# One fused attention and mixture-of-experts kernel: transposing transfers moved behind the maxima's, stacking and splitting of maxima moved forward, gates copied six steps behind a fetch

## The chip, the cores and the metric

The kernel runs on one NeuronCore of a Trainium2 chip, as one launch. The metric is the device time of that launch in microseconds, lower is better. Three runs of the kernel before took 1018.86, 1014.24 and 1013.54 us; their median, 1014.24 us, is the time before. One more execution was taken by the hardware profiler and took 1015.18 us. All profile lines below are from that one.

A core has five engines with an instruction queue each, worked off in order: PE (TensorE, matmuls; its weight loads are shown as PEld), DVE (VectorE), ACT (ScalarE), POOL (GpSimd) and SP (SyncE, which here only issues transfers). ACT and POOL issue transfers too. All transfers share 16 DMA engines.

## The reference

The inputs are `q`, `k` and `v` of 8 batches, 8 heads, 576 tokens and 64 features, a scalar `tau` = 0.02, and the gate and expert weights.

```python
scores = scale * np.matmul(q, k.transpose(0, 1, 3, 2))
thresh = np.max(scores, axis=-1, keepdims=True) - tau
scores = np.where(scores >= thresh, scores, -1000000000.0)
attn   = softmax(scores);  out = np.matmul(attn, v)
x      = out.transpose(0, 2, 1, 3).reshape(4608, 512)
expert_idx = np.argmax(x @ w_gate, axis=1)        # one of 8 experts
y[t] = gate_w[t] * relu(x[t] @ w1[expert]) @ w2[expert]
```

So each row of scores keeps only the entries within `tau` of its maximum, and each of the 4608 tokens goes to one of 8 experts, whose hidden layer is 1024 wide. The row maximum must be exact enough that the comparison keeps the same entries, and the choice of the expert must not flip. Therefore the operands are split into pairs of half-precision numbers (a high part and a rest) that are multiplied together.

## The kernel before

**Attention.** The work is cut into 32 pairs of heads, four pairs to a batch, and each pair into 10 steps. One step of the program issues, for a pair `n`, a unit of transposed scores (`st`, lines 335 and 336) with exponential (ACT) and mask (DVE), for an earlier pair a piece of attention times values (`av`, lines 408 to 419), and for a later pair a unit of plain scores (`s`, lines 286 and 288), of which DVE takes the negated row maxima (`nm`, lines 293 and 298). The plain scores run 20 steps ahead of the transposed ones.

**Maxima.** When a pair's plain scores are done, `parts` reduces the maxima to `r` (line 305); three steps later PE transposes them (`pst`, line 309), and ACT and DVE in turn split them into three half-precision parts `ptT` (lines 314 to 317), one operation a step. Three small transfers on SP (line 323) put these parts as three more rows into `CQ`, one of the operands of line 336. So the first `st` unit of a pair can't start before they have landed. The tiles of `pst`, of the logits (`lg`), of the ranks (`rk`) and of the expert counts (`pc`) share one PSUM buffer.

**Stacking.** `split` makes high and low parts of a pair's q and k (ACT, then POOL for `lo`, line 223), and `stack` writes them with 13 transfers on SP (lines 237 to 252) into `QK`, `ck` and `CQ`, four buffers each. `SL` (8) sets how many steps ahead of the plain scores that happens; loading and splitting hang on the same number.

**Batch end and routing.** After a batch's fourth pair, `finish` sets up: transposing transfers of the batch's rows `R` on SP (line 499, `xTg`; four of them, and a fifth for the half block `Rh` of an odd batch), the logits (line 519) on PE, `route` (DVE, lines 526 to 554), `ranks` (lines 575 to 592), and then the sending of each block of rows to its place in DRAM by indirect transfers on POOL (line 596, `xs`). `R` has two buffers, so batch b+2 writes (ACT line 470, POOL line 467) into what batch b sends from.

**Experts.** `level` makes tables of rows on DVE after batches 5, 6 and 7. `fetch` (line 799) gathers a group's 128 rows from `xs` by an indirect transfer on POOL, transposes them by a transfer on SP (line 805, `xTm`), and copies the gate (DVE, line 808, `gt`) and the target row (POOL, line 813). Groups 0, 1 and 2 can be fetched after batch 5 and groups 3 and 4 after batch 6; from group 5 on, the sends of batch 7 must have been made. `gemm1` (line 850) and `gemm2` (line 877) do the expert's two layers, fed by weights that SP loads (line 752, `wf`) and ACT and DVE split (lines 765 and 766, `wb`).

**What sets the order.** `after(k, f, where)` puts an action k steps on, at one of three places (FRONT, MID, END) of the step; each engine gets its instructions in the order in which the steps emit them. That holds up to 16 steps before the end of the attention. What is emitted later is ordered by a scheduler's own estimate of time, and may be put among the last written-out steps.

Of the kernel before, what the change touches and what calls it, by code (L numbers as in the profile page):

```python
# [11 lines left out]
F32 = mybir.dt.float32  # L12
# [3 lines left out]
ALU = mybir.AluOpType  # L16
# [3 lines left out]
B, H, S, D = 8, 8, 576, 64  # L20
DM, E, F = 512, 8, 1024
# [22 lines left out]
CAP = NTOK  # L44

TUNE = dict(
    lead=10, cast=1, sl=8, ll=15, sp0=6, sps=0, lv=-9, sv=-2, av=2, tr=4, d=2, lg=5, d5=2, d6=2, d7=1, lg7=9, km=16, rate=15, dh=1, do=3, ws0=6, wsd=3, w1d=5, plv=1, xv=3, so=0, sto=0, ord=0, sc=5, fa=3, fd=4, wa1=-70, wa2=-86, wl1=-28, wl2=-6, avb=2, route=1, ranks=7, pp=8, ew=4, maskat=0, w1a=-40, w1b=3,
)


# [1 line left out]
def kernel(  # L52
# [9 lines left out]
    nc = tc.nc  # L62
# [9 lines left out]
    ew = ctx.enter_context(tc.tile_pool(name="ew", bufs=4))  # L72
# [8 lines left out]
    pp = apool.enter_context(tc.tile_pool(name="pp", bufs=5))  # L81
# [93 lines left out]
    FRONT, MID, END = range(3)  # L175

    def plan(k, f, where=END):
        assert (k, where) >= (now[0], slot[0])
        acts.setdefault(k, ([], [], []))[where].append(f)

    def after(k, f, where=END):
        plan(now[0] + k, f, where)

    def phase(p, least):

        return least + (p - now[0] - least) % NSTEP if now[0] + least < KM else least
# [113 lines left out]
    def parts(n):  # L300


        nm = st[n]["nm"]
        r = small.tile([P, 9], F32, tag="r", name=f"r_{n}")
        nc.vector.tensor_reduce(r, nm.rearrange("p a t -> p t a"), axis=AX.X, op=ALU.min)

        def turn():
            ps = ps_m.tile([P, 512], F32, tag="m", name=f"pst_{n}")
            nc.tensor.transpose(ps[0:9, 0:P], r, ident)
            x, y = ps[0:9, 0:P], ps[0:9, P:2 * P]  # L310
            t = small.tile([9, 3, P], F16, tag="ptT", name=f"ptT_{n}", bufs=1)
            v, a = nc.vector, nc.scalar
            for i, f in enumerate((
                lambda: a.activation(t[:, 0], x, AF.Identity, bias=thr[0:9]),
                lambda: v.scalar_tensor_tensor(y, x, thr[0:9], t[:, 0], ALU.add, ALU.subtract),
                lambda: a.copy(t[:, 1], y),
                lambda: (v.tensor_tensor(t[:, 2], y, t[:, 1], ALU.subtract), rows(t)),
            )):
                after(1 + i, f, MID)

        def rows(t):
            for p in range(3):
                nc.sync.dma_start(
                    st[n]["CQ"][64 + p:65 + p].rearrange("p (t c) -> p t c", t=9), t[:, p]
                )

        after(3, turn, FRONT)
# [57 lines left out]
    def row(b, j):  # L385
        return Rs[b % 2][:, j] if j < NT else Rh[b // 2 % 2]

    def halves(x):
        return x.bitcast(F16).rearrange("p (c h d) -> p c h d", c=4, h=2)
# [35 lines left out]
    def divide(x, y, rs, eng):  # L425
        wait = int(eng is nc.gpsimd)
        nc.scalar.activation(rs, y[..., D:W].squeeze(y.ndim - 1), AF.Copy, bias=EPS)
        after(wait, lambda: nc.vector.reciprocal(rs, rs))
        after(2 * wait, lambda: eng.tensor_tensor(
            x, y[..., 0:D], rs.unsqueeze(rs.ndim).to_broadcast(list(x.shape)), ALU.mult  # L430
        ))
# [43 lines left out]
    def finish(b):  # L475
        last = b == B - 1
        n = NT + b % 2
        xTs = {}

        def lone():  # L480
            o = halves(Rh[b // 2 % 2][:, 0:DM])
            y = xhs[b // 2 % 2]
            rs = small.tile([P, H], F32, tag="rsh", name=f"rsh_{b}", bufs=1)
            xn = xp.tile([P, H, D], F32, tag="xn", name=f"xnh_{b}", bufs=2)
            x = xn.rearrange("p (c u) d -> p c (u d)", c=4)
            eng = nc.vector if last else nc.gpsimd
            divide(xn, y, rs, eng)

            def high():
                nc.scalar.copy(o[:, :, 0], x)  # L490
                after(1, lambda: eng.tensor_tensor(o[:, :, 1], x, o[:, :, 0], ALU.subtract))

            after(1 if last else 4, high)

        def turn(j):
            if j % 2 == 0:
                xTs["t"] = rpool.tile([P, 2, 8, P], F16, tag="xT", name=f"xTg_{b}_{j}", bufs=3)
            xTs[j] = xT = xTs["t"][:, j % 2]
            nc.sync.dma_start_transpose(xT, row(b, j)[:, 0:DM].bitcast(F16))

        if n > NT:
            after(1 if last else 2, lone)
        t0 = 2 if last else TUNE["tr"] + 3
        for j in range(n):
            after(t0 + j, lambda j=j: turn(j))
        d = t0 + n - 1
        dist = TUNE[f"d{b}"] if b >= B - 3 else TUNE["d"]
        after(
            d + TUNE["lg7"] if last else phase(7, d + TUNE["lg"]), lambda: logits(b, n, xTs, dist),
            END if last else FRONT,  # L510
        )
# [256 lines left out]
    def late(m):  # L768
        return m == "x" or m >= NEARLY

    def fetch(m):

        idx, bad, par = slots[m]
        g, i = group_of[m] if m != "x" else ((m,), 0)
        if m in range(NF, NF + 2):

            Rm = row(B - 2, m - NF)
            at = 4 * ROW - (2 - (m - NF)) * DM
            xT = Rs[B % 2].rearrange("p j c -> p (j c)")[:, at:at + DM].bitcast(F16)
            xT = xT.rearrange("p (i c t) -> p i c t", i=1, c=8)  # L780
        elif m in range(NF):
            Rm = pools[0].tile([P, ROW], I32, tag="Rm", name=f"Rm_{m}", bufs=2)
            xT = pools[0].tile([P, 1, 8, P], F16, tag="xTm", name=f"xTm_{m}", bufs=NF)
        else:
            Rm = row(B - 1, 0 if m == "x" else m % 5)
            if i == 0:
                xT = rpool.tile([P, 2, 8, P], F16, tag="xT", name=f"xTm_{m}", bufs=3)
            else:
                xT = ms[g]["xT"]
        if i == 0:  # L790
            ms[g] = dict(xT=xT, par=par, gw=[], ti=[])
        d = ms[g]
        for z in range(1 + late(m)):
            dst = xT[:, i]
            if late(m):
                Rm = row(B - 1, z if m == "x" else (2 * m + z) % 5)
                dst = xT.rearrange("p i c t -> p (i c t)")[:, 0:8 * PL].rearrange("p (c t) -> p c t", c=8)
                d["xT"], dst = dst, dst[:, :, P * z:P + P2 * z]
            dma = nc.gpsimd.indirect_dma_start(
                Rm, None, xs[:, :], bass.IndirectOffsetOnAxis(ap=idx[:, z:z + 1].bitcast(U32), axis=0)  # L800
            )
            for x in sends:
                tc.add_manual_dep(dma.ins, x.name, SYNC)
            tc.add_to_no_dep_group("xs", dma.ins)
            nc.sync.dma_start_transpose(dst, Rm[0:P2 if z else P, 0:DM].bitcast(F16))
            gt = small.tile([P, 2], I32, tag="gt", name=f"gt_{m}_{z}", bufs=6)
            gw, ti = gt.bitcast(F32)[:, 0:1], gt[:, 1:2]
            nc.vector.tensor_copy(gw, Rm.bitcast(F32)[:, DM:DM + 1])
            to = Rm[:, DM + 1:DM + 2]
            if z:  # L810
                nc.gpsimd.tensor_tensor(ti, to, to, ALU.add)
                to = ti
            nc.gpsimd.tensor_tensor(ti, to, bad[:, z:z + 1], ALU.add)
            d["gw"].append(gw)
            d["ti"].append(ti)

# [162 lines left out]
    def tables0():  # L979
        T[0], _ = level(0, ((), EARLY[0]), None)  # L980
        for m in range(NF):
            after(1 + m, lambda m=m: fetch(m))

    def tables1():
        T[1], _ = level(1, EARLY, T[0])
        for m in range(2):
            after(1 + m, lambda m=m: fetch(NF + m))
# [43 lines left out]
    for i in range(8):  # L1031
        plan(k + WS0 + WSD * i, lambda i=i: split_w(*wseq[i]))
        if i + 2 < 8:
            plan(k + WS0 + WSD * i, lambda i=i: load_w(*wseq[i + 2]))
    TABLES = {B - 3: tables0, B - 2: tables1, B - 1: tables2}
    plan(KEND + 12, close)

# [26 lines left out]
    for e in range(1, E + NL):  # L1064
        for w in range(2):
            for c in range(4):
                i = 4 * w + c
# [11 lines left out]
    turn = [8]  # L1079
# [88 lines left out]
    with tc.For_i(NL, total) as m:  # L1168
        idx = small.tile([P, 2], I32, tag="idx", name="idx_x", bufs=1)
        nc.vector.tensor_copy(idx.unsqueeze(1), T["row"][:, ds(m, 1)])  # L1170
        bad = small.tile([P, 2], I32, tag="badx", name="bad_x", bufs=1)
# [66 lines left out]
```

## Time and profile before

| What | Value |
|---|---|
| Median of three runs | 1014.24 us |
| Profiled execution, whole time | 1015.18 us |
| Its span, first to last instruction | 1013.0 us |
| Mean TensorE clock that was granted | 0.977 of full |
| PE busy with matmuls | 927.9 us |
| DVE, ACT, POOL busy | 652.6, 611.4, 556.5 us |
| HBM traffic over the span | 108 GB/s |

A timeline row gives the start, the duration, the engine, the line, the operation with output and inputs, and in brackets how long the engine stood idle before and what released it. "SPq" and "ACTq" are transfers being issued by the queue of SP or ACT; their duration is the time of issue, not of the transfer. A row of the waits reads: engine and line, what it waited for, the total in us, how often, and the longest. A row of the windows gives, for a stretch of time, the busy us and the number of instructions of each engine, the granted clock of PE (1.00 is full speed), the busy share of the DMA engines and GB/s.

### The profile page before, as it was taken

What the parts mean: (1) busy time and instruction counts of PE and PEld (TensorE: products, weight loads), DVE (VectorE), ACT (ScalarE), POOL (GpSimd) and SP (SyncE); (2) the same over time, 40 slices, a digit from 0 to 9 for tenths busy, and PEclk for the clock granted to TensorE, in tenths of its full rate; (3) what the DMA queues carried; (4) which work ended last, traced back from release to release, by engine and by line L of the source; (5) the groups of instructions that cost most, each with busy time, mean ns of one, the idle gap of its engine ahead of it and who ended that gap; (6) DMA issues with size and microseconds to landing.
All of it is one profiled execution on the core that took longest, in us unless ns stands there. A gap on an engine that the chain in (4) does not pass through costs nothing. (4 is left out here: it accounts for less than half of the span.)

```text
span 1013.0 us, 25162 instructions
## 1 busy us (share of the span) xinstructions
PE 927.9 (92%) x10027; PEld 657.6 (65%) x10027; DVE 652.6 (64%) x1309; ACT 611.4 (60%) x1036; POOL 556.5 (55%) x477
## 2 busy tenths in 40 slices
PE   2799999989999799899798699699999999999997
PEld 1266767657767567676576587387766676667684
DVE  6798888868888688888687675725341433423550
ACT  2588888858888678788587564324342433423641
POOL 5378788958979779789585671441212122122121
PEclk9899999989999899999899899899999999999999
DMA  6554474754746646647446749988564755557720
GB/s 174 134 122 108 110 166 118 164 122 130 171 112 161 130 115 174 147 127 163 113 127 154 123 167 286 313 176 225 173 175 153 228 154 172 156 158 219 226 104 26
DMA packets 181715, 158.96 MB, mean 157 GB/s; under 512 B 137561, under 2 KB 153947, under 8 KB 181596
## 3 DMA queue, kind: packets, MB, share of 16 engines
q1 hardware_dynamic: 129244, 100.35, 40.0%
q10 hardware_dynamic: 43200, 27.53, 10.6%
q0 software_dynamic: 9152, 29.45, 8.8%
q8 instruction: 80, 1.31, 0.6%
q14 instruction: 39, 0.32, 0.1%
HBM read 90.24 MB, written 19.44 MB: 108 GB/s over the span
## 5 line engine op out<-in xcount | busy, mean ns | idle before, releaser
L372 POOL TENSOR_TENSOR pl<-e,ph 128x1024 f16<-128x1024 f32 x95 | 204.8, 2157 | 63.4 <-ACT ph L371 61.9
L298 DVE TENSOR_REDUCE nm<-s 128x1 f32<-128x512 f32 (+1 forms) x320 | 200.1, 636 | 61.0 <-PE s L288 59.1
L850 PEld LDWEIGHTS <-wb 128*128 128x128 f16 x2304 | 190.2, 99 | 29.3 <-issue 11.4
L850 PE MATMUL h<-xTm,wb 128*128 128x256 f16 (+2 forms) x2112 | 196.7, 255 | 10.1 <-DMA xTm<-R 10.1
L877 PE MATMUL y<-wb,hl 128*128 128x512 f16 (+1 forms) x1056 | 201.5, 360 | 0.0
L363 ACT ACTIVATE e<-st,ntau 128x512 f32<-128x512 f32 x192 | 130.8, 683 | 55.3 <-PE st L336 53.4
L877 PEld LDWEIGHTS <-hl 128*128 128x128 f16 (+1 forms) x1056 | 94.1, 100 | 98.1 <-issue 1.9
L286 PE MATMUL s<-QK 128*128 128x512 f16 (+3 forms) x640 | 138.2, 293 | 14.2 <-DMA QK<-lo 13.5
L766 DVE SCALAR_TENSOR_TENSOR wb<-wf,wb 128x1024 f16<-128x1024 f32 x96 | 116.7, 1252 | 52.0 <-ACT wb L765 49.6
L336 PE MATMUL st<-CQ,ck 128*128 128x512 f16 (+3 forms) x640 | 133.7, 290 | 16.3 <-DMA CQ<-ptT 16.3
L288 PE MATMUL s<-ck,CQ 128*128 128x512 f16 (+3 forms) x640 | 142.6, 291 | 4.8 <-DMA ck<-lo 4.4
L335 PE MATMUL st<-QK 128*128 128x512 f16 (+3 forms) x640 | 138.4, 293 | 8.6 <-DVE e L348 6.4
L366 DVE SCALAR_TENSOR_TENSOR e<-st,e 128x512 f32<-128x512 f32 x192 | 129.7, 676 | 8.6 <-ACT e L363 5.8
L891 POOL DMA_INDIRECT out_dram<-o,gt x40 | 43.6, 1089 | 150.1 <-ACT o L888 139.4
L347 ACT ACTIVATE e<-st,ntau_f 128x512 f32<-128x512 f32 (+1 forms) x160 | 93.5, 602 | 53.6 <-PE st L336 53.4
L838 ACT ACTIVATE hl<-h 128x512 f16<-128x512 f32 (+1 forms) x80 | 45.8, 573 | 125.3 <-PE h L850 125.3
L414 PE MATMUL av<-vf,e 128*128 128x65 f32 (+1 forms) x1024 | 118.7, 254 | 0.0
L765 ACT ACTIVATE wb<-wf 128x1024 f16<-128x1024 f32 x96 | 97.4, 1049 | 19.8 <-PE h L850 8.8
L348 DVE SCALAR_TENSOR_TENSOR e<-st,e 128x512 f32<-128x512 f32 (+1 forms) x160 | 91.6, 589 | 20.2 <-ACT e L347 20.1
L414 PEld LDWEIGHTS av<-vf,e 128*128 128x128 f32 (+1 forms) x1024 | 104.0, 167 | 0.4
L371 ACT CAST ph<-e 128x1024 f16<-128x1024 f32 x96 | 99.3, 1034 | 1.7 <-DVE e L366 1.7
L417 PE MATMUL av<-vop,ph 128*128 128x64 f16 x768 | 97.4, 194 | 0.0
(193 smaller groups left out, 1493.3 us busy)
## 6 DMA issues: line engine op xcount, KB each, us to landing
wf<-in_w_dram SPq DMA_DIRECT2D x96, 512.0 KB
qkf<-in_qk_dram ACTq DMA_DIRECT2D x30, 576.0 KB
vf<-in_v_dram ACTq DMA_DIRECT2D x30, 320.0 KB
QK<-hi SPq DMA_DIRECT2D x64, 144.0 KB
QK<-hi SPq DMA_DIRECT2D x64, 72.0 KB
QK<-lo SPq DMA_DIRECT2D x64, 72.0 KB
ck<-lo SPq DMA_DIRECT2D x64, 72.0 KB
CQ<-hi SPq DMA_DIRECT2D x64, 64.0 KB
```

The costliest lines, as they stand in the source:

```text
L286: nc.tensor.matmul(sc[rows, oc], d["QA"][a][:, cols], d["KB"][a][:, CH[c]], start=True, stop=False)
L288: nc.tensor.matmul(sc[rows, oc], d["CQ"][:, at:at + cols.stop - cols.start], d["CK"][a][:, CH[c]], start=False, stop=True,)
L298: nc.vector.tensor_reduce(o, sc[:, 0:width(t)], axis=AX.X, op=ALU.max, negate=True)
L335: nc.tensor.matmul(sc[rows, oc], d["KB"][a][:, cols], d["QA"][a][:, CH[c]], start=True, stop=False)
L336: nc.tensor.matmul(sc[rows, oc], d["CK"][a][:, cols], d["CQ"][:, q], start=False, stop=True)
L363: nc.scalar.activation(pf, sc, AF.Exp, bias=ntau, scale=0.125 / SS)
L366: nc.vector.scalar_tensor_tensor(pf, sc, 0.0, pf, ALU.is_ge, ALU.mult)
L372: (nc.vector if (n, t) in PLV else nc.gpsimd).tensor_tensor(l, pd, h, ALU.subtract)
L414: nc.tensor.matmul(av[rows, a], d["Pf"][t][:, q], vf[:, tv], start=False, stop=last)
L766: nc.vector.scalar_tensor_tensor(o[:, :, 1], x, SW, o[:, :, 0], ALU.mult, ALU.subtract)
L850: nc.tensor.matmul(o, Wt[:, c, wh, f], x, start=c == 0 and z == 0, stop=c == 3 and z == 2,)
L877: nc.tensor.matmul(o, h[:, hh], Wt[:, f, wh, c], start=f == 0 and z == 0, stop=f == 7 and z == 2)
```

## The change

Six numbers and places are changed, in four functions.

```diff
-    lead=10, cast=1, sl=8, ll=15, ...
+    lead=10, cast=1, sl=10, ll=15, ...
@@ parts.turn: the four operations that split the maxima
-                after(1 + i, f, MID)
+                after(i, f, MID)
@@ finish
-        t0 = 2 if last else TUNE["tr"] + 3
+        t0 = 2 if last else 14 if b < B - 3 else 7
         for j in range(n):
-            after(t0 + j, lambda j=j: turn(j))
-        d = t0 + n - 1
+            after(t0 + (j // 2 if t0 == 14 else j), lambda j=j: turn(j))
+        d = t0 + ((n - 1) // 2 if t0 == 14 else n - 1)
@@ fetch
-            nc.vector.tensor_copy(gw, Rm.bitcast(F32)[:, DM:DM + 1])
-            to = Rm[:, DM + 1:DM + 2]
-            if z:
-                nc.gpsimd.tensor_tensor(ti, to, to, ALU.add)
-                to = ti
-            nc.gpsimd.tensor_tensor(ti, to, bad[:, z:z + 1], ALU.add)
+            def where(Rm=Rm, gw=gw, ti=ti, z=z):
+                nc.vector.tensor_copy(gw, Rm.bitcast(F32)[:, DM:DM + 1])
+                ...
+                nc.gpsimd.tensor_tensor(ti, to, bad[:, z:z + 1], ALU.add)
+            if m == "x":
+                where()
+            else:
+                after(6, where)
@@ tables0, the fetches of groups 0, 1 and 2
-            after(1 + m, lambda m=m: fetch(m))
+            after(1 + 4 * m, lambda m=m: fetch(m))
```

Loading, splitting and stacking of a pair come two steps earlier; the split of the maxima and their transfers one step earlier. For batches 0 to 4 the transposing transfers come seven steps later, two to a step, and through `d` the logits, the routing and the sends of these batches come ten steps, one pair, later. Batches 5, 6 and 7 keep theirs. The first three fetches are four steps apart and not one, and the copies of gate and target come six steps after their fetch. The lines behind `fetch` move down by seven numbers in the changed kernel.

**SP, at the end of batch 1.** `CQ` with `ptT` are the maxima's rows, `xTg` the transposing transfers (`R_210` and `Rh_211` are the rows of batch 1), and `CQ` with `before` is the first of a stack's 13 transfers. Before:

```order
L323 DMA CQ_163<-ptT_3140 1x9x128 x3
L499 DMA_TRANSPOSE xTg_0_3374<-R_210 128x8x128 x2
L499 DMA_TRANSPOSE xTg_2_3426<-R_210 128x8x128 x2
L237 DMA CQ_162<-before 3x18x64
L243 DMA QK_0_3466<-hi_3323 64x1152
...
L252 DMA CQ_162<-hi_3323 64x64
L499 DMA_TRANSPOSE xTg_4_3480<-Rh_211 128x8x128
L323 DMA CQ_164<-ptT_3452 1x9x128 x3
L237 DMA CQ_163<-before 3x18x64
```

And in the changed kernel:

```order
L323 DMA CQ_163<-ptT_3151 1x9x128 x3
L237 DMA CQ_162<-before 3x18x64
L243 DMA QK_0_3424<-hi_3250 64x1152
...
L252 DMA CQ_162<-hi_3250 64x64
L323 DMA CQ_164<-ptT_3461 1x9x128 x3
L499 DMA_TRANSPOSE xTg_0_3601<-R_210 128x8x128 x2
L499 DMA_TRANSPOSE xTg_2_3633<-R_210 128x8x128 x2
L499 DMA_TRANSPOSE xTg_4_3660<-Rh_211 128x8x128
L237 DMA CQ_163<-before 3x18x64
```

All five transposing transfers now stand behind the next pair's maxima and ahead of the stack after that; before, four stood ahead of one stack and the fifth behind it.

**DVE, at the first fetches.** `gt` is the gate's copy, `Rm` the fetched rows, `e` and `st` the masks of the transposed scores that PE waits for, and line 305 the reduction for the last pair's maxima. Before:

```order
L808 COPY gt_0_9877<-Rm_9873 128x1
L348 SCALAR_TENSOR_TENSOR e_6_9862<-st_6_9859,e_6_9862 128x512
L298 TENSOR_REDUCE nm_9599<-s_7_9893 128x1
L305 TENSOR_REDUCE r_9897<-nm_9599 128x9
L808 COPY gt_0_9904<-Rm_9900 128x1
L348 SCALAR_TENSOR_TENSOR e_6_9862<-st_7_9889,e_6_9862 128x512
```

And in the changed kernel:

```order
L810 COPY gt_0_9881<-Rm_9877 128x1
L305 TENSOR_REDUCE r_9899<-nm_9603 128x9
...
L348 SCALAR_TENSOR_TENSOR e_8_10010<-st_8_10005,e_8_10010 128x512
L810 COPY gt_0_9965<-Rm_9961 128x1
L348 SCALAR_TENSOR_TENSOR e_10_10017<-st_10_10012,e_10_10017 128x64
L317 TENSOR_TENSOR ptT_9951<-pst_9949,ptT_9951 9x128
L810 COPY gt_0_10119<-Rm_10115 128x1
L348 SCALAR_TENSOR_TENSOR e_8_10010<-st_9_10036,e_8_10010 128x512
```

The second copy now stands behind six masks that it stood ahead of (the three dots leave out nine rows, five of them such masks), and the third, which stood 10 rows behind the second, follows it by three.

**SP, behind the last pair.** `R_210` and `Rh_212` are now the rows of batch 7, `R_209` takes the fetched rows of groups 3 and 4, and `wf` are the weights. Before:

```order
L752 DMA wf_3_0_10980<-in_w_dram 128x1024
L752 DMA wf_0_1_11000<-in_w_dram 128x1024
L499 DMA_TRANSPOSE xTg_0_10798<-R_210 128x8x128 x2
L805 DMA_TRANSPOSE R_209<-R_209 128x8x128
L499 DMA_TRANSPOSE xTg_2_10821<-R_210 128x8x128 x2
L805 DMA_TRANSPOSE R_209<-R_209 128x8x128
L499 DMA_TRANSPOSE xTg_4_10830<-Rh_212 128x8x128
```

And in the changed kernel:

```order
L752 DMA wf_0_0_10853<-in_w_dram 128x1024
L499 DMA_TRANSPOSE xTg_0_10794<-R_210 128x8x128 x2
L499 DMA_TRANSPOSE xTg_2_10819<-R_210 128x8x128 x2
L499 DMA_TRANSPOSE xTg_4_10830<-Rh_212 128x8x128
L752 DMA wf_1_0_10896<-in_w_dram 128x1024
L752 DMA wf_3_0_10980<-in_w_dram 128x1024
L805 DMA_TRANSPOSE R_209<-R_209 128x8x128 x2
```

Three weight loads fewer stand ahead of the five transfers for batch 7's logits, and the two fetched groups' transposing transfers no longer stand between them. This is the scheduler's part of the program; no line of the diff names it.

More of the change, by code (lines that the diff above doesn't have):

```diff
@@ L46 @@
 TUNE = dict(
-    lead=10, cast=1, sl=8, ll=15, sp0=6, sps=0, lv=-9, sv=-2, av=2, tr=4, d=2, lg=5, d5=2, d6=2, d7=1, lg7=9, km=16, rate=15, dh=1, do=3, ws0=6, wsd=3, w1d=5, plv=1, xv=3, so=0, sto=0, ord=0, sc=5, fa=3, fd=4, wa1=-70, wa2=-86, wl1=-28, wl2=-6, avb=2, route=1, ranks=7, pp=8, ew=4, maskat=0, w1a=-40, w1b=3,
+    lead=10, cast=1, sl=10, ll=15, sp0=6, sps=0, lv=-9, sv=-2, av=2, tr=4, d=2, lg=5, d5=2, d6=2, d7=1, lg7=9, km=16, rate=15, dh=1, do=3, ws0=6, wsd=3, w1d=5, plv=1, xv=3, so=0, sto=0, ord=0, sc=5, fa=3, fd=4, wa1=-70, wa2=-86, wl1=-28, wl2=-6, avb=2, route=1, ranks=7, pp=8, ew=4, maskat=0, w1a=-40, w1b=3,
 )
@@ L807, in fetch @@
             gw, ti = gt.bitcast(F32)[:, 0:1], gt[:, 1:2]
-            nc.vector.tensor_copy(gw, Rm.bitcast(F32)[:, DM:DM + 1])
-            to = Rm[:, DM + 1:DM + 2]
-            if z:
-                nc.gpsimd.tensor_tensor(ti, to, to, ALU.add)
-                to = ti
-            nc.gpsimd.tensor_tensor(ti, to, bad[:, z:z + 1], ALU.add)
+            def where(Rm=Rm, gw=gw, ti=ti, z=z):
+                nc.vector.tensor_copy(gw, Rm.bitcast(F32)[:, DM:DM + 1])
+                to = Rm[:, DM + 1:DM + 2]
+                if z:
+                    nc.gpsimd.tensor_tensor(ti, to, to, ALU.add)
+                    to = ti
+                nc.gpsimd.tensor_tensor(ti, to, bad[:, z:z + 1], ALU.add)
[3 more added lines that the diff above has]
+                after(6, where)
             d["gw"].append(gw)
```

## Prediction

> **What bounds the kernel now.** I read the page's first line, then the windows of the two stages, then what PE waited for.
>
> ```profile
> span 1013.0 us, 25162 instructions
> 50.00:600.00 550.00, 507.45 (x6557) 368.45 (x6556) 444.36 (x934) 431.64 (x792) 438.68 (x288) 0.98 0.58 135
> 675.00:1000.00 325.00, 325.00 (x2490) 226.83 (x2488) 128.48 (x167) 129.93 (x171) 66.35 (x90) 1.00 0.58 171
> ```
>
> PE sets the time. Of the experts' stage from 675 us on it has every microsecond, at full clock, so nothing is to be had there. In the attention it stands idle for 550 - 507 = 43 us, and the next engines, DVE, POOL and ACT, are busy for 78 to 81% only. What can be won is idle time of PE, and slow clock behind it. The waits of PE say for what it stood:
>
> ```profile
> PE st L336 <- DMA CQ<-ptT: 16.3, 13, 6.4
> PE lg L519 <- DMA xTg<-Rh: 13.3, 3, 4.7
> PE h L850 <- DMA xTm<-R: 10.1, 1, 10.1
> PE st L335 <- DVE e L348: 6.4, 1, 6.4
> PE lg L519 <- DVE ptT L317: 2.3, 6, 0.4
> PE rk L575 <- DVE ptT L317: 2.3, 6, 0.4
> PE pc L955 <- DVE ptT L317: 1.2, 1, 1.2
> ```
>
> Each of these rows names something that the change moves. The long ones cost more than their idle time; the timeline of PE and the windows behind the idle times show it:
>
> ```profile
> 212.84 0.38 PE L519 MATMUL lg<-wg,xTg 128*128 128x16 f16 x8 [4.07 <-DMA xTg<-Rh]
> 351.74 0.38 PE L519 MATMUL lg<-wg,xTg 128*128 128x16 f16 x8 [4.70 <-DMA xTg<-Rh]
> 491.04 0.38 PE L519 MATMUL lg<-wg,xTg 128*128 128x16 f16 x8 [4.54 <-DMA xTg<-Rh]
> 564.01 0.64 PE L335 MATMUL st<-QK 128*64 128x512 f16 x2 [6.43 <-DVE e L348]
> ```
> ```profile
> 212.80:219.40 6.60, 6.55 (x38) 4.06 (x39) 2.84 (x8) 2.93 (x5) 2.37 (x1) 0.50 0.31 90
> 351.70:355.90 4.20, 4.17 (x25) 2.48 (x26) 1.44 (x3) 1.82 (x3) 1.07 (x1) 0.50 0.39 124
> 564.00:567.60 3.60, 3.59 (x32) 2.72 (x31) 3.60 (x4) 1.21 (x3) 3.46 (x3) 0.51 0.40 75
> 658.90:663.00 4.10, 4.06 (x39) 4.06 (x39) 2.97 (x16) 0.00 (x0) 3.42 (x8) 0.50 0.95 231
> ```
>
> Behind each, PE runs for 3.6 to 6.6 us at a granted clock of 0.50. Half of such a stretch is lost too: 3.3, 2.1, 1.8 and 2.1 us.
>
> **The change part by part.**
>
> *Logits of batches 1 and 3.* SP at the end of batch 1:
>
> ```profile
> 194.53 5.44 SPq L499 DMA_TRANSPOSE xTg<-R  x4
> 209.28 1.71 SPq L499 DMA_TRANSPOSE xTg<-Rh  x1
> 211.11 2.49 SPq L323 DMA_DIRECT2D CQ<-ptT  x3
> ```
>
> The fifth transfer stands behind a whole stack and is issued at 209.28, after PE has come to the logits (212.84 - 4.07 = 208.8). In the changed order all five are issued in one go, some ten steps ahead of the logits. A step is 1.63 us: line 336 begins a pair at 98.95 and again, six pairs on, at 196.67 (rows below), and 97.7 / 60 = 1.63. Five issues at 5.44 / 4 = 1.36 us are 6.8 us, and from issue to use the fifth took 212.84 - 209.28 = 3.6 us, together 10.4 of 16 us: hidden. Gain 4.07 + 3.3 + 4.70 + 2.1 = **14.2 us** (bounds 0 and 14.2). Batch 5 is left out of the new place: its five transfers and the stack have the same total of issues ahead of the logits, so its 4.54 us and slow clock stay. Nothing on the way to the end needs the routing of batches 0 to 4 ten steps sooner; what it runs into is the third rival.
>
> *Waits for the maxima's split on DVE.* Line 317 comes a step, 1.63 us, sooner, which is more than each of the thirteen waits behind it (0.4 and 1.2). Gain 2.3 + 2.3 + 1.2 = **5.8 us** (bounds 0 and 5.8).
>
> *Waits for the maxima's rows.*
>
> ```profile
> 37.08 0.58 PE L336 MATMUL st<-CQ,ck 128*128 128x512 f16 x1 [6.45 <-DMA CQ<-ptT]
> 98.95 0.38 PE L336 MATMUL st<-CQ,ck 128*128 128x512 f16 x1 [1.48 <-DMA CQ<-ptT]
> 196.67 0.38 PE L336 MATMUL st<-CQ,ck 128*128 128x512 f16 x1 [0.66 <-DMA CQ<-ptT]
> 33.35 2.54 SPq L323 DMA_DIRECT2D CQ<-ptT  x3
> ```
>
> The first, 6.45, stays: its rows (33.35) stand behind the same two stacks on SP as before. The other twelve make 16.3 - 6.45 = 9.9 us, 0.8 each. One step sooner takes nearly all of that, provided SP is free; it is, as the stack ahead, too, starts earlier. But behind the new place of the transposing transfers a stack and the next rows still queue: five issues of 1.36 us on SP push them by up to 6.8 us. I take 8.5 of 9.9 (bounds 0 and 9.9).
>
> *Fetches and gates.* Before the last pair:
>
> ```profile
> 552.59 0.98 POOL L799 DMA_INDIRECT Rm<-xs,row  x1 [0.68 <-issue]
> 555.33 1.30 SPq L499 DMA_TRANSPOSE xTg<-R  x1
> 563.20 0.15 DVE L808 COPY gt<-Rm 128x1 f32<-128x1 f32 x1 [9.97 <-DMA Rm<-xs,row]
> 577.76 0.36 PE L519 MATMUL lg<-wg,xTg 128*128 128x16 f16 x8 [1.70 <-DMA xTg<-R]
> ```
>
> DVE stands for 9.97 us at the second gate's copy, with the masks behind it; PE runs on until its score buffers are full and then waits 6.43 us. The fourth transposing transfer of batch 6, kept behind the fetches on SP, costs another 1.70. In the changed order the copy stands behind six masks and that transfer ahead of the second fetch's, so at most 6.43 + 1.8 + 1.70 = 9.9 us go. But the fetch too starts later, and the last pair's rows now stand behind its transposing transfer on SP: what was DVE's wait may in part be SP's. PE reaches those six masks about six steps on; they hold scores and values of one pair only, and from 553 to 557.6 us (564.01 - 6.43) PE did four of them, so DVE comes to the copy near 559. A fetch that is issued near 555 and takes the same 10.6 us (552.59 to 563.20) lands near 566; less what the buffers cover (four units, 4.6 us) some 3 us of new idle time stay. Gain **7 us** (bounds 0 and 9.9). The Trainium skill, in "TensorE: Matmul & The Clock Gate", section "HAM oscillation", says that the clock falls only behind idle gaps over about 3.4 us; the trace agrees so far (1.70 us left it at 1.00, 4.07 us did not), and by that rule these 3 us cost no clock.
>
> *Last batch.* PE uses up the groups that it has at 648.9 us (658.94 - 10.07) and waits for group 5, which needs batch 7's rows sent:
>
> ```profile
> 605.71 6.35 SPq L499 DMA_TRANSPOSE xTg<-R  x2
> 612.22 1.23 SPq L805 DMA_TRANSPOSE R<-R  x1
> 618.50 1.83 SPq L499 DMA_TRANSPOSE xTg<-Rh  x1
> 623.83 0.25 DVE L526 TENSOR_REDUCE lg<-lg 128x40 f32<-128x80 f32 x1 [6.91 <-PE lg L519]
> 639.38 0.16 DVE L588 CAST posi<-rk 128x5 int32<-128x5 f32 x1
> 658.94 1.33 PE L850 MATMUL h<-xTm,wb 128*128 128x128 f16 x11 [10.07 <-DMA xTm<-R]
> L766 DVE SCALAR_TENSOR_TENSOR wb<-wf,wb 128x1024 f16<-128x1024 f32 x96 | 116.7, 1252 | 52.0 <-ACT wb L765 49.6
> ```
>
> The fifth transfer was issued at 618.50. In the changed order nothing stands between the five: 605.71 + 4 x 1.36 = 611.2, 7.3 us sooner. From the logits' sum (623.83) to the places (639.38) DVE has one weight split (line 766) and not eight, 7 x 1.25 = 8.8 us less. Together 16 us, more than the 10.07 wanted; but SP still puts weight loads ahead of group 5's transfer, so I take 10 of 10.07 + 2.1 = 12.1 us (bounds 0 and 12.1).
>
> *Stacking two steps sooner* costs nothing by itself: the same instructions, on ACT and POOL at 78 to 80%. For new small waits (POOL at batch ends, SP behind the transposing transfers) I put down **3 us**, between 0 and 10.
>
> **Sum.** 14.2 + 5.8 + 8.5 + 7 + 10 - 3 = 42.5 us off the profiled execution's 1015.2 (2.2 us around its span) gives 972.7. That execution was 0.9 us over the median; **973 us** is my forecast, 4.1% less.
>
> **The rivals.**
>
> *Last batch unchanged.* Group 5 is fetched sooner, but weight loads fill the DMA engines and SP, and its transposing transfer lands when it did. For it: even behind the wait (658.9 to 663 us above) the DMA engines are busy for 0.95. Against it: five weight loads fewer stand ahead of that transfer. 973 + 10 = 983.
>
> *Second fetch later.* It was 10.6 us under way with three transposing transfers issued around it; now up to five and a weight load are ahead. If it lands 5 us later still (two more transfers of 1.36 us and the load; an estimate), DVE and the last pair's rows wait for it and the gain of 7 falls to about 0, with slow clock: 982. The Trainium skill, "DMA: Bandwidth & Descriptors", section "Queues, rings and completion order", speaks for it: a completion mark is written only after all earlier writes of that DMA engine, across its queues. No row here shows the mark apart from the data.
>
> *Slower: the sends meet the next writer.*
>
> ```profile
> 255.96 1.03 POOL L596 DMA_INDIRECT xs<-R,posi  x1 [0.15 <-issue]
> 279.61 0.61 ACT L470 CAST R<-xn 128x512 f16<-128x512 f32 x1
> xs<-R,posi POOLq DMA_INDIRECT x32, 3.8
> 175.00:200.00 25.00, 24.28 (x277) 17.01 (x276) 21.63 (x41) 22.83 (x42) 24.35 (x17) 1.00 0.62 161
> ```
>
> Batch 1's last send of `R` is issued at 255.96 and read out by 255.96 + 1.0 + 3.8 = 260.8; batch 3 writes the same buffer at 279.61. One pair, 16.3 us, later leaves 2.5 us. POOL is busy for 24.35 of 25 us where sends lie, and for even batches the odd batch's half block now falls there as well. If POOL falls behind by more than 2.5 us, ACT stands at line 470 with all exponentials behind it, five times. At 10 us each with the clock, 50 us: 973 + 50 = 1023. Against it: POOL has slack in the pairs between, and 8.5 us each would be needed to lose the whole gain.
>
> *The change doesn't do what it says:* the five transfers land late in their new place too, and batches 1 and 3 wait as before: 973 + 14 = 987.
>
> **How the numbers follow.** Forecast 0.55, last batch unchanged 0.18, second fetch later 0.14, slower 0.08, late transfers 0.05. The lower end takes every term at its upper bound: 14.2 + 5.8 + 9.9 + 9.9 + 12.1 = 51.9, so 1014.2 - 51.9 = 962. The upper end has two rivals at once with the small waits near their bound: 973 + 10 + 9 + 3 = 995. About 2 in 10 lie outside, most of it above. A difference under 0.5% (5 us) can't be told from none. Only the slower rival comes near 1014; half of it lies beyond. So faster 0.92, same 0.04, slower 0.04.
>
> **What would show it.** Right: no idle time of PE at line 519 for `Rh` but the one of batch 5 (4 to 5 us), so slow clock in four places and not seven; no waits for line 317; waits for `ptT` under 8 us with the first; at group 5 under 3 us; PE above 95% from 50 to 600 us. Wrong: DVE or SP standing over 6 us at the second fetch; ACT waiting at line 470 for `xs`; the logits of batches 1 or 3 waiting; PE idle over 5 us near 640 us.

## The result and the profile after

The changed kernel took 983.19 us (median of four runs, 979.54 to 984.16), against 1013.89 us before: a ratio of 0.969, with a 95% interval of 0.967 to 0.972. So 3.1% went, where 4.1% (973 us) was forecast; the time lies inside the range of 962 to 995. Run again later beside other kernels, it gave 982.67 us and 0.970 (0.968 to 0.972). Two executions of kernels below are left out of their times: one of 1012.85 us at a granted clock of 0.938, and one of 3302 us in which the matmuls took some three times as long everywhere.

The profiled execution took 984.16 us. The first two lines of its page, the windows of attention, changeover and experts, and what PE waited for (total, times, longest):

```profile
span 982.1 us, 25201 instructions
PE 924.7 (94%) x10027; PEld 655.2 (67%) x10027; DVE 643.2 (65%) x1309; ACT 618.6 (63%) x1036; POOL 557.6 (57%) x477
```
```profile
50.00:600.00 550.00, 527.90 (x6842) 384.70 (x6842) 452.49 (x976) 450.50 (x813) 442.42 (x295) 0.98 0.62 146
600.00:660.00 60.00, 56.92 (x642) 41.44 (x639) 35.55 (x95) 24.99 (x34) 29.01 (x30) 0.97 1.02 293
```
```profile
PE lg L519 <- DMA xTg<-R: 9.5, 4, 6.5
PE st L336 <- DMA CQ<-ptT: 8.9, 3, 6.6
PE st L335 <- DVE e L366: 5.8, 5, 2.4
PE y L884 <- DVE hl L846: 2.6, 2, 2.1
PE pst L309 <- DVE run L554: 1.7, 5, 0.4
PE pst L309 <- DVE pos L592: 1.4, 1, 1.4
PE h L857 <- DMA xTm<-R: 0.5, 1, 0.5
```

PE is now busy for 528 of 550 us and not 507. The two long waits for `Rh`, all thirteen behind line 317, all but two of the twelve short ones for `ptT`, the 6.43 us at the gate's copy and the 10.07 us at group 5 are gone in this execution. New or longer are the waits for batch 5's transposing transfers (line 519, now `R` first) and for masks of line 366.

Added up over windows of 1 us from 20 to 700 us, PE's idle time fell from 60.7 to 33.1 us, but what it loses at a low clock (busy time times one minus the granted clock) only from 13.9 to 13.1 us. Together that is 28.4 of the 30.9 us by which the span is shorter. The prediction's terms hold between 5.4 us of slow clock (batches 1 and 3) and 9.3 us (with the gate's copy and group 5), so of the 11.6 us that are missing against its 42.5, some 5 to 8 lie in the clock: six places ran slowly before, and six do after, only other ones.

At the end of batch 1, SP did what the change says:

```profile
203.66 2.45 SPq L323 DMA_DIRECT2D CQ<-ptT  x3
206.21 6.30 SPq L499 DMA_TRANSPOSE xTg<-R  x4
212.61 1.56 SPq L499 DMA_TRANSPOSE xTg<-Rh  x1
214.27 0.81 SPq L237 DMA_DIRECT2D CQ<-before  x1
220.71 1.15 PE L519 MATMUL lg<-wg,xTg 128*128 128x16 f16 x40
```

Rows of the maxima, then all five transposing transfers, then the stack; the logits run without a break. Batch 5, which keeps its old place, got worse. SP and PE there:

```profile
451.10 2.63 SPq L499 DMA_TRANSPOSE xTg<-R  x2
453.82 1.56 SPq L237 DMA_DIRECT2D CQ<-before  x1
464.15 0.60 SPq L252 DMA_DIRECT2D CQ<-hi  x1
464.79 2.69 SPq L499 DMA_TRANSPOSE xTg<-R  x2
467.58 1.27 SPq L499 DMA_TRANSPOSE xTg<-Rh  x1
468.12 0.38 PE L519 MATMUL lg<-wg,xTg 128*128 128x16 f16 x8 [6.55 <-DMA xTg<-R]
```

Two transfers go ahead of the stack (its first and last issues are shown, 453.82 and 464.15) and three behind it. PE stands for 6.55 us, then 1.00 and 0.83 more: 8.4 us, where it was 4.54.

The first fetches and the last batch, on PE, SP and DVE:

```profile
510.48 0.38 PE L335 MATMUL st<-QK 128*128 128x512 f16 x1 [1.61 <-DVE e L366]
531.05 0.38 PE L335 MATMUL st<-QK 128*128 128x512 f16 x1 [2.36 <-DVE e L366]
550.36 0.36 PE L519 MATMUL lg<-wg,xTg 128*128 128x16 f16 x8 [1.63 <-DMA xTg<-R]
580.20 8.47 SPq L499 DMA_TRANSPOSE xTg<-R  x4
588.77 1.26 SPq L499 DMA_TRANSPOSE xTg<-Rh  x1
592.97 0.25 DVE L526 TENSOR_REDUCE lg<-lg 128x40 f32<-128x80 f32 x1 [2.77 <-PE lg L519]
601.59 0.17 DVE L588 CAST posi<-rk 128x5 int32<-128x5 f32 x1
626.09 4.12 PE L857 MATMUL h<-xTm,wb 128*128 128x128 f16 x71 [0.50 <-DMA xTm<-R]
```

In place of the 6.43 us at the gate's copy and the 1.70 us at batch 6's logits stand three waits of 1.6 to 2.4 us. This differs from execution to execution: in the second profiled one of the same kernel (981.72 us) the third fetch, issued at 542.65 us, took 6.3 us and not 3.6, and DVE again stood at a gate's copy, with PE behind it:

```profile
548.99 0.15 DVE L810 COPY gt<-Rm 128x1 f32<-128x1 f32 x1 [5.88 <-DMA Rm<-xs,row]
549.79 0.42 PE L335 MATMUL st<-QK 128*128 128x512 f16 x1 [4.61 <-DVE e L348]
```

So the stall at the copy is shorter, but not gone for good. In the last batch the five transfers are in one piece, and from the logits' sum to the places DVE takes 8.6 us where it took 15.6; group 5 is waited for 0.50 us.

### The profile page after: what moved, and what is told of

Its sections match the earlier page's. It is cut to its first block, busy times and chain, and to the rows that moved or that the text cites. A ratio compares the mean times of both kernels' runs of the same rounds, so it can differ in the third digit from the quotient of the medians.

```text
span 982.1 us, 25201 instructions
## 1 busy us (share of the span) xinstructions
PE 924.7 (94%) x10027; PEld 655.2 (67%) x10027; DVE 643.2 (65%) x1309; ACT 618.6 (63%) x1036; POOL 557.6 (57%) x477
## 5 line engine op out<-in xcount | busy, mean ns | idle before, releaser
L298 DVE TENSOR_REDUCE nm<-s 128x1 f32<-128x512 f32 (+1 forms) x320 | 202.2, 635 | 27.6 <-PE s L288 24.3
L418 PE MATMUL av<-vop,pl 128*128 128x65 f16 x768 | 96.9, 194 | 0.0
```

The costliest lines, as they stand in the source:

```text
L298: nc.vector.tensor_reduce(o, sc[:, 0:width(t)], axis=AX.X, op=ALU.max, negate=True)
```

## The experiments

The question was which part brought what, since the prediction gave each part a term of its own. Three parts meet on SP: the **transfers** (transposing transfers of batches 0 to 4 later), the **stack** (two steps sooner) and the **split** (maxima's split and rows one step sooner); the fourth is the **fetches**.

**Each part alone, on the kernel before.** The transfers alone:

```diff
-        t0 = 2 if last else TUNE["tr"] + 3
+        t0 = 2 if last else 14 if b < B - 3 else 7
...
-        d = t0 + n - 1
+        d = t0 + ((n - 1) // 2 if t0 == 14 else n - 1)
```

> The kernel before with one part of the change alone: the transposing transfers of batches 0 to 4 seven steps later, two to a step, and logits, routing and sends ten steps later. Theory A (as the prediction's sum has it, each part worth its own term): no wait at line 519 for Rh in batches 1 and 3, 14.2 us less, 1013 - 14 = 999 us. Theory B (the parts hang together on SP: without the sooner split, two of the transfers stand ahead of the maxima's rows in SP, as in the run with the late split, where PE then waited 1.9 to 2.4 us for ptT at the ends of batches): five such waits take back some 10 us, 1009 us.

1024.37 us, a ratio of 1.008 (1.005 to 1.011): slower, and even more than theory B had it. SP and PE at the end of batch 0:

```profile
138.38 2.72 SPq L499 DMA_TRANSPOSE xTg<-R  x2
141.55 2.49 SPq L323 DMA_DIRECT2D CQ<-ptT  x3
144.09 2.65 SPq L499 DMA_TRANSPOSE xTg<-R  x2
147.95 0.59 PE L336 MATMUL st<-CQ,ck 128*128 128x512 f16 x1 [3.17 <-DMA CQ<-ptT]
```

The waits for `Rh` in batches 1 and 3 are gone, but without the sooner split the rows stand between the transfers, and PE waits for `ptT` at the end of each of the five batches: 3.17, 3.57, 2.17, 3.84 and 2.51 us, four of them with slow clock behind. Batch 5's wait grew to 5.40 us, and group 5's was still 7.68 us.

The split alone:

```diff
-                after(1 + i, f, MID)
+                after(i, f, MID)
```

> The kernel before with the split of the maxima, and with it their rows' transfers, one step sooner, and nothing else of the change. Theory A (this part has its own worth): the thirteen waits behind line 317 go (5.8 us), and of the 9.9 us of waits for ptT behind the first some 7: 1013 - 13 = 1000 us. Theory B (the rows stand behind a stack on SP, and that stack is not sooner): the waits behind line 317 go, those for ptT stay: 1013 - 6 = 1007 us.

1002.71 us, 0.991 (0.988 to 0.993). The waits behind line 317 are gone, and those for `ptT` fell from 16.3 to 11.2 us; theory B is out on that. The three waits for `Rh` became longer (13.3 to 17.6 us), since PE comes to the logits sooner by more than their fifth transfer does: in batch 1 PE was there 4.5 us sooner (204.28 and not 208.78), the transfer was issued 3.0 us sooner (206.25 and not 209.28). And the 10 us at group 5 are gone here too (0.2 us left), though nothing of the last batch was touched, so the time, which holds that too, doesn't decide between the theories:

```profile
PE lg L519 <- DMA xTg<-Rh: 17.6, 3, 7.0
PE st L336 <- DMA CQ<-ptT: 11.2, 8, 6.4
PE h L850 <- DMA xTm<-R: 0.2, 1, 0.2
```

The stack alone:

```diff
-    lead=10, cast=1, sl=8, ll=15, ...
+    lead=10, cast=1, sl=10, ll=15, ...
```

> The kernel before with loading, splitting and stacking two steps sooner, and nothing else of the change. Theory A (the stack takes SP's queue ahead of the transposing transfers): two of the four or five transfers stand ahead of the stack and the rest behind it in all six batches; PE waits 6 to 8 us for the logits of each, as in the run with the old transfers, and runs slower behind it; 1032 there, and 13 us more for the late split: 1045 us, slower than before by 3%. Theory B (stacking sooner costs nothing by itself, as the prediction has it): 1005 to 1014 us.

1046.22 us, 1.032 (1.030 to 1.034), as theory A had it to 1 us. SP and PE at the end of batch 0, and PE's waits for all batches:

```profile
128.50 2.74 SPq L499 DMA_TRANSPOSE xTg<-R  x2
131.33 0.83 SPq L237 DMA_DIRECT2D CQ<-before  x1
140.81 2.93 SPq L499 DMA_TRANSPOSE xTg<-R  x2
144.46 0.38 PE L519 MATMUL lg<-wg,xTg 128*128 128x16 f16 x8 [4.56 <-DMA xTg<-R]
PE lg L519 <- DMA xTg<-R: 39.8, 13, 6.7
```

Now the stack cuts every batch's transfers in two, as it does batch 5's in the changed kernel.

**Each part taken out of the changed kernel.** The transfers back (`t0 = 2 if last else 7`):

> The changed kernel with the transposing transfers of batches 0 to 4 back in their old place, seven steps after the batch's end and one a step; the stack stays two steps sooner. Theory A (only two of the transfers stand ahead of that stack, as at batch 5 of the changed kernel): every batch waits as batch 5 did, 7.5 to 8.4 us and about 3.5 us of slow clock: 983 + 5 x 11.5 = 1040 us, slower than before. Theory B (batch 5's wait came from the loads around it, not from the place): batches 1 and 3 wait as before, 983 + 14 = 997 us.

1031.63 us, 1.015 (1.011 to 1.019). Theory A: the waits of line 519 for `R` are 42.7 us in 14 places, with the fifth transfers' 2.4 us beside them. A batch costs some 9 to 10 us ((1031.63 - 983.19) / 5 = 9.7; by the two ratios 9.2), less than the 11.5 put down.

The stack back (`sl=8`):

> The changed kernel with loading, splitting and stacking back at 8 steps ahead (and with it the first expert's weights, which hang on the same number). Theory A (stacking sooner earned nothing by itself, and cost at batch 5 and at the first weights): batch 5's wait falls from 8.4 back to 4.5 us, its slow clock by 1.5 us, and the wait of 1.6 us at 510 us with its slow clock (1.7 us) goes; 983 - 5.4 - 3.3 = 974 us. Theory B (stacking sooner is what makes SP free for the maxima's rows): the rows stand behind the stack again, waits of PE for ptT come back to some 16 us in about 13 places, and the time is 983 + 7 - 5 = 985 us or more.

988.51 us, 0.976 (0.971 to 0.980). Theory B: the waits for `ptT` are back. Of theory A only the wait at 510 us is gone; batch 5's did not shrink to 4.5 us, it is 7.4 us for `Rh` alone, so both theories were too kind there:

```profile
PE st L336 <- DMA CQ<-ptT: 18.1, 11, 6.5
PE lg L519 <- DMA xTg<-Rh: 7.4, 1, 7.4
```

The split back (`after(1 + i, f, MID)`):

> The changed kernel with the split of the maxima, and so their rows' transfers, one step later, as before. Theory A (the one step is what removed both kinds of waits): the twelve waits of 0.38 us and the one of 1.2 us behind line 317 are back (5.8 us), and so are the waits for ptT (7.4 us): 983 + 13 = 996 us. Theory B (the waits for ptT went because the stack comes sooner and the transposing transfers stand elsewhere): only 5.8 us come back, and less where the logits now come at other steps: 983 + 6 = 989 us or less.

997.58 us (median of three), 0.984 (0.977 to 0.990). Theory A: 2.8, 2.3 and 1.5 us behind line 317, and 14.8 us for `ptT`, four of its waits at ends of batches (2.42, 1.91, 2.40, 1.12 us), because the rows again stand between transposing transfers, as with the transfers alone.

The fetches back (one step apart, copies right behind):

```diff
-            after(1 + 4 * m, lambda m=m: fetch(m))
+            after(1 + m, lambda m=m: fetch(m))
...
-            if m == "x":
+            if True:
                 where()
```

> The changed kernel with the first three fetches one step apart and the copies of gate and target right behind each fetch, as before. Theory A (as predicted: the copy that waits for its fetch blocks the masks): DVE stands at a copy for about 10 us, PE waits 6.4 us for a mask and runs 1.8 us slower behind it: 983 + 8 = 991 us. Theory B (this part of the change earned nothing, since after it PE idles for 2.4, 1.6 and 1.0 us at 531 to 552 us, with slow clock behind, where it idled in one piece): within 3 us of 983.

984.65 us (median of four), 0.974 (0.970 to 0.978), which can't be told from the changed kernel's 0.969 and 0.970. The profile of the same kernel, taken in another execution:

> The same kernel as the one with the old fetches, for a profile (its first one was taken while the chip held TensorE at a third of its pace). Its times alone, 982 to 989 us, speak for no difference. Theory A (the copy blocks the masks): DVE stands some 10 us at a copy, PE waits over 6 us for a mask near 545 us, and something else is better by as much. Theory B: with the other parts of the change the copies no longer block, since the fetches start where DMA engines and SP are free; DVE stands under 4 us at a copy.

988.10 us. POOL's second fetch and DVE's copies there:

```profile
534.27 0.98 POOL L799 DMA_INDIRECT Rm<-xs,row  x1 [0.61 <-issue]
539.01 0.15 DVE L810 COPY gt<-Rm 128x1 f32<-128x1 f32 x1 [4.04 <-DMA Rm<-xs,row]
546.85 0.15 DVE L810 COPY gt<-Rm 128x1 f32<-128x1 f32 x1 [3.24 <-DMA Rm<-xs,row]
```

The copy still blocks DVE, but the fetch took 4.7 us here (534.27 to 539.01) and not 10.6, so it blocks for 4.04 us, and no single wait of PE at a mask in that stretch is over 2.4 us. That is no worse than the 4.61 us at a mask, behind 5.88 us at a copy, in the second execution of the changed kernel. With the other parts in place this one is worth at most a few us, and the runs don't show that it is worth any.

All of it together, ratios to the kernel before:

| Part | alone | changed kernel without it |
|---|---|---|
| transfers later | 1.008 (1.005 to 1.011) | 1.015 (1.011 to 1.019) |
| stack sooner | 1.032 (1.030 to 1.034) | 0.976 (0.971 to 0.980) |
| split sooner | 0.991 (0.988 to 0.993) | 0.984 (0.977 to 0.990) |
| fetches apart | not run alone | 0.974 (0.970 to 0.978) |
| whole change | 0.969 (0.967 to 0.972) | |

Two of the three parts on SP cost time alone, and the three alone sum to 3% slower; together, without the fetches' part, they are 2.6% faster (0.974).

**Batch 5's transfers ahead of the stack.** This is the changed kernel with one more edit:

```diff
-            after(t0 + (j // 2 if t0 == 14 else j), lambda j=j: turn(j))
+            after(t0 + (j // 2 if t0 == 14 else min(j // 2, 1) if b == B - 3 else j), lambda j=j: turn(j))
```

> The changed kernel, with one thing more: the five transposing transfers of batch 5 are emitted two in one step and three in the next, so that all five stand ahead of the next pair's stack on SP; its logits stay where they are. Theory A (order of issue on SP): in the changed kernel only two of the five stood ahead of that stack, because the stack comes two steps sooner; PE waited 6.55 + 1.00 + 0.83 = 8.4 us for them and ran on at half clock for some 3.8 us of loss. With all five ahead these waits fall under 1 us: 983 - 12 = 971 us. Theory B (the transfers are late because the DMA engines are full at that place, 0.84 busy in the 5 us ahead): the transfers are slow in the new place too and the stack comes later, so PE waits for the next scores instead; gain under 4 us, 979 to 984.

979.97 us, 0.969 (0.966 to 0.973). SP and PE:

```profile
451.52 7.81 SPq L499 DMA_TRANSPOSE xTg<-R  x4
459.43 1.31 SPq L499 DMA_TRANSPOSE xTg<-Rh  x1
463.30 0.36 PE L519 MATMUL lg<-wg,xTg 128*128 128x16 f16 x8 [1.11 <-DMA xTg<-R]
465.77 0.39 PE L519 MATMUL lg<-wg,xTg 128*128 128x16 f16 x8 [2.11 <-DMA xTg<-Rh]
```

The order of issue was the cause: 8.4 us of waiting became 3.2 us. Theory A's 12 us did not come: 5.2 us of waiting and 0.5 us of slow clock went (3.1 us lost and not 3.5), and a change of that size lies at the limit of what the runs can tell (0.969 for both kernels).

**Two further tries on top of that.** First, the tables' 15 small DVE operations in three pieces, a step apart:

> The kernel with batch 5's five transfers ahead of the stack, and further the 15 small operations of the first tables (DVE, after batch 5) emitted in three pieces a step apart, with masks between them; the first fetches come two steps later for that. Theory A (PE waits 2.4 us for a mask that stands behind these 15 operations in one piece, and runs 3 us slower behind it): both go, 980 - 5 = 975 us. Theory B (the masks are as late, since DVE has the same work there and is busy throughout): the idle time is spread over smaller waits, and the time stays at 978 to 982 us.

980.33 us, 0.964 (0.960 to 0.968). The wait for masks at 526 us went, but the tables hold the PSUM buffer longer that the maxima's transposition needs, and PE waits there instead:

```profile
531.25 0.28 PE L309 MATMUL pst<-ident,r 128*9 128x128 f32 x1 [3.40 <-DVE row L627]
541.41 0.78 PE L519 MATMUL lg<-wg,xTg 128*128 128x16 f16 x24 [3.16 <-DVE ptT L317]
```

Second, the split of q and k one step later and the first expert's weights at their old steps:

```diff
-    ..., sp0=6, ...
+    ..., sp0=5, ...
-    k = NSTEP * (NPAIR - 2) - LEAD - SL
+    k = NSTEP * (NPAIR - 2) - LEAD - 8
```

> The kernel with batch 5's five transfers ahead of the stack, and two things more: each pair's split into high and low parts one step later (so that on POOL the low part of R of line 467 comes ahead of the 2.4 us of line 223), and the first expert's weights at their old steps, two later than in the changed kernel. Theory A: batch 5's transfers start 2.4 us sooner, its waits of 1.1 + 2.1 us and most of the 3.1 us of slow clock go, and so does the wait for the first weight split (1.2 us at 505 us): 980 - 6 = 974 us. Theory B (the later weights stand in the way of batch 6's transposing transfers and the last batch instead): 980 to 985 us.

981.84 us, 0.968 (0.965 to 0.971). Batch 5's waits fell to 1.4 and 1.1 us and the one for the first weights is gone, but the next pair's rows, behind five transfers and a stack, are late by more than that:

```profile
477.42 0.58 PE L336 MATMUL st<-CQ,ck 128*128 128x512 f16 x1 [5.23 <-DMA CQ<-ptT]
```

Beside it the changed kernel was run again:

> The changed kernel itself once more, on the same chip as the others of this group, for the comparison: 981 to 985 us.

It gave the 982.67 us told above. Of the three tries, only the one with the tables in pieces has an interval that may lie below the changed kernel's, by half a per cent; it ran in another group, so whether it is really faster stays open.

## Why the prediction was right, and where it was wrong

- **What bounds the kernel**: right. PE sets the time, the gain is idle time of the attention and the changeover, and the experts' stage gave nothing.
- **Logits of batches 1 and 3 (14.2 us)**: right in size. Both waits and the slow clock behind them (5.3 us by the windows of 1 us) are gone, 14.1 us. Wrong was to book them to the later transfers alone, which by themselves made the kernel 9 us slower (1024.37 against 1015.67 beside it).
- **Waits behind line 317 (5.8 us)**: right, all gone. Some 1.2 us came back as longer waits of the maxima's transposition (line 309), which belongs to the 3 us put down for small waits.
- **Waits for the maxima's rows (8.5 us)**: 7.4 us (16.3 to 8.9). The reason given, that the stack ahead starts earlier too, was right: with the stack back at its old place these waits come back, though the split is sooner.
- **"Its five transfers and the stack have the same total of issues ahead of the logits"** (batch 5): this step failed. The total is the same, but not the order. The stack came sooner by two steps, batch 5's transfers did not, and so three of five moved behind it: 8.4 us of waiting for 4.54, and 3.5 us of slow clock for 2.4, 5 us lost. The place was read for batches 0 to 4, whose order the change states, and only summed for batch 5.
- **"Stacking two steps sooner costs nothing by itself: the same instructions"**: this failed for the same reason. Alone it costs 33 us (1046.22 against 1013.54 beside it), the largest effect of any part alone. ACT and POOL were looked at for cover; the queue on which the stack lies is SP, where a stack (13 issues, 453.82 to 464.75 in the rows above), the rows (2.45) and five transfers (6.30 + 1.56) are together more than a pair's 16.3 us.
- **Fetches and gates (7 us)**: 1.6 us in the profiled execution. From 537 to 578 us before, PE idled for 11.2 us (without the 1.24 behind line 317, counted above) and lost 1.8 us to the clock; in that place after (503 to 556) it idles for 6.3 us (without 1.00 for the rows, counted above) and loses 5.1. In the second execution it idles there for 9.9 us and loses 3.1, as much as before. The second fetch was not later but quicker, 5.9 us from 537.48 to 543.33, so that rival did not come; a third fetch that lands late, as in the second execution, was not thought of. In place of the stall at the copy stand three small waits in the profiled execution: DVE at the first weight split (508.60, behind weights that hang on the same number as the stack and so also came two steps sooner, which the prediction overlooked), DVE in the 15 operations of the tables (526.96 to 530.4; before, the wait behind them was 1.09 us and not 2.36), and batch 6's logits. That the number `SL` moves the weights was shown by the stack put back, which puts them back too, and by the last try: in both the wait at 505 to 510 us goes.
- **Last batch (10 us)**: 7.5 us. The working was right: five transfers in one piece, 5.7 us sooner against PE's last matmul of the attention (588.77 - 577.66 now, 618.50 - 601.71 before), and one weight split in DVE's way, 6.9 us less. Group 5's wait went, but waits of 3.1 us in all up to 634 us (its own 0.50 among them) and a slow stretch of 1.6 us took its place. It can't be booked to one part of the change: the waits for group 5 and those behind it (`xTm`) are gone with the split alone and at most 2.3 us with any one part left out, but 7.7 us with the transfers alone and 12.5 us with the stack alone. The order there is the scheduler's, and it changes with whatever stands before.
- **"By that rule these 3 us cost no clock"**: wrong, see below.
- **The signs**: two more did not come. Slow clock was to be left in four places and not seven; between 20 and 700 us it is in six, as before. The waits for `ptT` were to be under 8 us; they are 8.9.
- **The last step of the sum**: 972.7 us was for the profiled execution, which lay 0.9 us over the median; the forecast of the median should have been 971.8 and not 973.

The measured terms sum to 14.1 + 5.8 + 7.4 + 1.6 + 7.5 - 5 - 2.1 = 29.3 us, of 31; the last term is line 309 (1.6 us) and 0.5 us more of slow clock behind the first rows. The 13 us between this and 42.5 are the fetches (5.4), batch 5 (5), the last batch (2.5) and the rows (1.1), less 0.9 that the small waits took less than put down. The time is that of two rivals (982 and 983), but neither is what happened. The slower rival, sends that meet the next writer, did not come: no wait for `xs` stands in ACT's list at line 470.

## What to carry to other kernels

Where several edits move work on one in-order queue, their effects do not add: write down the order of the blocks on that queue at every place where they meet, for the instances that the edit does not touch too, and ask which block is due first. Here stack, rows and transposing transfers at a batch's end take more than a pair's time on SP, so a block that moves ahead of another delays it by its whole length. And when a stall is removed from a chain that has little slack, count the next two small stalls in its place, with their slow clock.

## What the runs showed of the hardware

The granted clock falls behind shorter idle times than expected. In the changed kernel it was at 0.53 to 0.57 after gaps of 1.61, 2.36 and 1.63 us (the last with 1.00 us more behind it); in the kernel before, a gap of 1.71 us at 425.9 left it at full:

```profile
511.00:515.00 4.00, 3.99 (x25) 2.39 (x23) 3.96 (x8) 3.64 (x5) 2.26 (x2) 0.57 0.60 191
531.50:535.00 3.50, 3.49 (x22) 2.23 (x20) 3.50 (x6) 2.31 (x4) 1.00 (x3) 0.53 0.38 83
552.20:556.00 3.80, 3.80 (x29) 3.19 (x29) 2.70 (x7) 0.69 (x1) 3.80 (x3) 0.56 0.31 57
```
```profile
426.00:430.00 4.00, 4.00 (x38) 2.64 (x38) 3.21 (x7) 2.78 (x7) 1.59 (x2) 1.00 0.61 136
```

What decides is how much idle time falls into one stretch of 3.41 us. In each of thirteen traces of this case, the starts of the slow spells lie whole multiples of 3.413 us apart, to 0.003 us (in the changed kernel 33.33, 463.41, 511.20, 531.68, 552.16 and 634.08 us: 126, 14, 6, 6 and 24 such stretches), and each spell before the kernel's end lasts one, two, three or four of them (28, 30, 17 and 3 of 78). Cut into stretches at these borders, from 20 us on, the traces show: of the stretches at full clock with over 1.75 us of idle PE, 71 of 71 were followed by a slow one; with 1.40 to 1.75 us, 7 of 30; with 1.0 to 1.40 us, none of 60; with less, none of 3332. So about half a stretch is the limit. The gap of 1.61 us (508.87 to 510.48) and that of 1.71 us (424.19 to 425.90) each lie whole in one stretch, at the limit, where both outcomes are seen.

The Trainium skill, "TensorE: Matmul & The Clock Gate", section "HAM oscillation — how this bites in real kernels", puts the limit at idle gaps over about 3.4 us; the runs say that half of that can be enough. For a sum, by these counts: a gap of over 3.5 us has more than 1.75 us in one stretch wherever it falls, and is to be booked with a slow spell; one of 1.75 to 3.5 us may be split by a border and cost nothing more; and a spell costs up to 1.7 us for each of its stretches, half of 3.41. Here, breaking one long stall into several of about 2 us saved idle time and cost clock.
